# Moving the two layers' input tiles to the right end of SBUF, behind a 96-byte pad

## The chip, the cores and the metric

One core of a Trainium2 chip runs the kernel. The metric is device time in microseconds for one execution. The kernel before took 782.60, 784.05 and 780.63 us in three runs, so its median is 782.6 us. The profile is of one further execution.

## What is computed

Clustered attention, then two dense two-matrix layers. q, k and v have 2 batches, 8 heads, 768 positions and 64 values per head; 16 centroids per head decide which key a query may see.

```python
mask = q_assign[:, :, :, None] == k_assign[:, :, None, :]      # nearest centroid of q and of k
scores = np.where(mask, scale * np.matmul(q, k.transpose(0, 1, 3, 2)), -1e9)
attn = softmax(scores)
x = np.matmul(attn, v)            # laid out as [1536 tokens, 512]
h = x @ w_in                      # layer 0: 512 -> 2048
x = softplus(h) @ w_out           #          2048 -> 512
h = x @ w_in2                     # layer 1
out = (h * clip(h + 3, 0, 6) / 6) @ w_out2
```

The weights arrive as 64-bit floats and the kernel turns them into pairs of 32-bit numbers. Inputs of products are held as a high and a low part (`hi`, `lo`), and each product is the sum of three matmuls: hi by hi, lo by hi, hi by lo.

## The kernel before, in words

**Attention** (lines 173 to 846) goes over 8 pairs of heads, 12 tiles of 128 queries each. For each pair TensorE first makes the similarities to the centroids (`p_sims`, L308: 12 matmuls of 384 columns into `psm`; the stationary operand is a 128-column slice of `cwh` or `cwl`, the moving one half of `hiq`, `loq`, `hik` or `lok`). Then, tile by tile, come the scores (L408), the transposes (L438) and the product with v (L453). The order of everything is written out by hand (`at(step, place, function)`), inside `tc.manual_schedule()`. The result lands in the eight tiles `xhi0..3` and `xlo0..3` (L73, L74), each 128 partitions by 1536 floats: the layers' inputs.

**The layers** go over 2 layers x 3 blocks of 512 tokens (`tb`) x 16 slices of 128 hidden units (`f`). One step is an h group (`phase_a`, L169: 4 x 3 = 12 matmuls of 512 columns; stationary the weight slice `pi` of this f, moving `xhi` or `xlo`) and then the y group of two steps earlier (`phase_b`, 12 matmuls of 512 columns). In layer 0 (L898) the y group has the weight slice `po` as stationary operand and `ghi`, `glo` (the activations) as moving one; in layer 1 (L900) it is the other way round, with `po` moving. So TensorE's order is h(f), y(f-2), h(f+1), y(f-1) and so on. VectorE and ScalarE convert the weights of each f about two steps ahead in layer 0 (L109 to L144), and during the last block of layer 0 and the start of layer 1 for layer 1.

**Where tiles lie.** A tile pool takes its space as a stack, from the left (low addresses) or, with `side="right"`, from the right end. The offsets in each partition that the allocator gives are these; the last column is the offset modulo 64 bytes, called the phase below.

| tiles | opened at | side | bytes from .. to | phase |
|---|---|---|---|---|
| `ident` and small constants | L58 | left | 16,512 .. 17,408 | 0 for `ident` |
| `xhi0..3`, `xlo0..3`, 6,144 each | L59 | left | 17,408 .. 66,560 | 0 |
| weights f = 0..2 (`wpa`), 4,096 a tile | L61 | left | 66,560 .. 91,136 | 0 |
| `ghi`, `glo`, `g`, `u` | L852 | left, after attention | 91,136 .. 113,664 | 0 |
| weights f = 7..15 (`wpc`) | L854 | left, after attention | 121,856 .. 195,584 | 0 |
| Q, K, `pr`, `vs`, `pth`, `ptl` | L178 to L181 | left, attention | 91,136 .. 171,008 | 0 |
| `cwh`, `cwl` | L224, L225 | left, attention | 191,200 .. 192,992 | 32 |
| `hiq`, `loq` (two buffers each) | L177 | right, attention | 195,552 .. 207,840 | 32 |
| `hik`, `lok` (two buffers each) | L177 | right, attention | 207,840 .. 220,128 | 32 |
| q, k, v as loaded | L176 | right, attention | 220,128 .. 229,344 | 32 |
| weights f = 3..6 (`wpb`) | L626 | right, once q, k, v are done | 196,576 .. 229,344 | 32 |

The right end is at byte 229,344, whose remainder by 64 is 32. All sizes of the large tiles are multiples of 64, so everything that is stacked from the right has phase 32.

GpSimd (POOL) fills constants first: the identity (`make_identity`, L64), `tiew` (L71, 16 memsets), `cwh`, `cwl`; TensorE's first work, 15 warm-up transposes (L245), waits for the identity.

Of the kernel before, what the change touches and what calls it, by code (L numbers as in the profile page):

```python
# [8 lines left out]
F32 = mybir.dt.float32  # L9
# [13 lines left out]
def cluster_attention_then_two_mlps(  # L23
# [12 lines left out]
    nc = tc.nc  # L36
    P = 128
# [18 lines left out]

    nc.scalar.preload_act_table_set("natural_log_exp_and_others")
    const = ctx.enter_context(tc.tile_pool(name="const", bufs=1))  # L58
    xpool = ctx.enter_context(tc.tile_pool(name="x", bufs=1))  # L59
    NFA, NFB = 3, 7  # L60
    wpa = ctx.enter_context(tc.tile_pool(name="wpa", bufs=1))  # L61

# [968 lines left out]
```

## Time and profile before

| what | value |
|---|---|
| median of three runs | 782.6 us (780.63 to 784.05) |
| span of the profiled execution | 782.9 us |
| TensorE busy, of the span | 765.8 us, 98% |
| VectorE, ScalarE, GpSimd busy | 457.5, 410.0, 150.6 us |
| granted TensorE clock, mean | 0.998 |

The page has busy times of each engine, the busy share in 40 slices, the DMA queues, the chain of work that ended last, and the costliest groups of instructions. A matmul's recorded duration overlaps the next one, because matmuls are pipelined: what one of them costs in a stream is the distance from its start to the next start. In the chain of waits, which is cut into pieces that follow one another, the length of a piece "x12" is therefore the cost of 12 matmuls.

### The profile page before, as it was taken

To read this page: it belongs to the slowest core of one execution; us is meant where nothing else is said; L and a number is where in the kernel's file an instruction comes from. 1 tells how busy PE (TensorE), PEld (TensorE's weight loads), DVE (VectorE), ACT (ScalarE), POOL (GpSimd) and SP (SyncE) were. 2 spreads that over 40 slices of the span, in tenths; PEclk is the share of its full clock that TensorE was granted. 3 is DMA by queue.
4 is the path that set the end of the run, shared out by engine and by line. 5 is a ranking of instruction groups with operands and counts; after the bars stand their busy time and mean duration, and the time that the engine had idled before them with its cause. 6 is when DMAs were issued, how large, how long until landed. Compare 5 with 4: busy or idle time off the path is not lost.

```text
span 782.9 us, 10593 instructions
## 1 busy us (share of the span) xinstructions
PE 765.8 (98%) x3841; PEld 645.2 (82%) x3841; DVE 457.5 (58%) x788; ACT 410.0 (52%) x815; POOL 150.6 (19%) x222
## 2 busy tenths in 40 slices
PE   7979999999999999999999999999999999999998
PEld 6778898899888788888888888888888888888886
DVE  5969889889888999721111276779842322232221
ACT  6869889888998766532121344546532322222222
POOL 3467568667444000000000000000000000000000
PEclk9999999999999999999999999999999999999999
DMA  6645676676573670000000355640000100010001
GB/s 189 171 128 135 175 193 170 160 191 158 113 202 119 220 285 1 1 1 0 1 1 27 108 192 184 206 144 0 1 1 0 54 1 0 1 54 0 1 1 54
DMA packets 40548, 71.32 MB, mean 91 GB/s; under 512 B 4752, under 2 KB 25648, under 8 KB 40496
## 3 DMA queue, kind: packets, MB, share of 16 engines
q1 hardware_dynamic: 40352, 70.52, 31.2%
q8 instruction: 30, 0.49, 0.3%
q14 instruction: 22, 0.18, 0.1%
q10 hardware_dynamic: 144, 0.13, 0.0%
HBM read 46.30 MB, written 3.19 MB: 63 GB/s over the span
## 4 chain that ended last, share of the span: by engine, by line
PE 88%; DVE 3%; DMA 2%; ACT 2%; POOL 2%; issue 1%; SPq 1%; POOLq 0%; ACTq 0%
PE h L169 32%; PE y L900 17%; PE y L898 16%; PE t L438 7%; PE pv L453 7%; PE s L408 6%; PE psm L308 2%; DMA row<-rT 1%; DVE nm L416 1%; DVE ptl L443 1%; DMA rsb<-row 1%; ACT pth L442 0%; DMA K<-lok 0%; PE warm L245 0%; DMA K<-hik 0%
## 5 line engine op out<-in xcount | busy, mean ns | idle before, releaser
L169 PE MATMUL h<-xhi,pi 128*128 128x512 f32 x768 | 238.5, 392 | 0.7 <-DVE pi L144 0.6
L169 PEld LDWEIGHTS h<-xhi,pi 128*128 128x128 f32 x768 | 143.7, 188 | 32.4 <-DVE pi L144 1.0
L879 DVE TENSOR_TENSOR glo<-g,ghi 128x512 fp32r<-128x512 f32 x96 | 66.4, 692 | 146.2 <-ACT ghi L866 117.4
L169 PE MATMUL h<-xlo,pi 128*128 128x512 f32 x384 | 150.0, 391 | 0.0
L900 PE MATMUL y<-po,ghi 128*128 128x512 f32 x384 | 118.9, 391 | 0.0
L898 PE MATMUL y<-ghi,po 128*128 128x512 f32 x384 | 118.8, 391 | 0.0
L443 DVE TENSOR_TENSOR ptl<-t,pth 128x384 fp32r<-128x384 f32 x192 | 97.7, 550 | 24.1 <-ACT pth L442 23.1
L872 DVE SCALAR_TENSOR_TENSOR g<-u,h 128x512 f32<-128x512 f32 x48 | 33.0, 687 | 127.2 <-ACT u L868 127.1
L868 ACT ACTIVATE u<-h,half 128x512 f32<-128x512 f32 x48 | 33.0, 687 | 128.3 <-PE h L169 128.0
L408 PE MATMUL s<-K,Q 128*128 128x256 f32 (+1 forms) x384 | 90.3, 356 | 6.5 <-ACT pr L424 3.9
L442 ACT ACTIVATE pth<-t 128x384 fp32r<-128x384 f32 x192 | 85.8, 491 | 15.6 <-PE t L438 14.7
L416 DVE TENSOR_REDUCE nm<-s 128x1 f32<-128x768 f32 x96 | 90.7, 945 | 2.9 <-PE s L408 2.9
L424 ACT ACTIVATE pr<-s,nm 128x768 f32<-128x768 f32 x96 | 86.9, 905 | 3.2 <-DVE nm L416 2.9
L438 PE MATMUL t<-ident,pr 128*128 128x128 f32 x576 | 85.9, 279 | 2.2 <-DVE ptl L443 1.8
L865 ACT ACTIVATE g<-h 128x512 f32<-128x512 f32 x48 | 28.5, 595 | 111.1 <-PE h L169 111.1
L169 PEld LDWEIGHTS h<-xlo,pi 128*128 128x128 f32 x384 | 72.0, 188 | 15.7
L900 PEld LDWEIGHTS y<-po,ghi 128*128 128x128 f32 x384 | 72.1, 188 | 15.6
L898 PEld LDWEIGHTS y<-ghi,po 128*128 128x128 f32 x384 | 72.0, 188 | 15.7
L408 PEld LDWEIGHTS s<-K,Q 128*128 128x128 f32 x384 | 65.8, 189 | 16.7 <-ACT pr L424 5.2
L438 PEld LDWEIGHTS t<-ident,pr 128*128 128x128 f32 x576 | 66.4, 141 | 15.7 <-DVE ptl L443 11.8
L900 PE MATMUL y<-po,glo 128*128 128x512 f32 x192 | 75.1, 391 | 0.0
L898 PE MATMUL y<-glo,po 128*128 128x512 f32 x192 | 75.0, 391 | 0.0
(126 smaller groups left out, 933.6 us busy)
## 6 DMA issues: line engine op xcount, KB each, us to landing
ri<-in_moe_w_in SPq DMA_DIRECT2D x29, 512.0 KB, 4.6
ro<-in_moe_w_out SPq DMA_DIRECT2D x29, 512.0 KB, 8.0
K<-hik SPq DMA_DIRECT2D x31, 192.0 KB, 5.1
Q<-hiq SPq DMA_DIRECT2D x15, 384.0 KB, 4.0
Q<-loq SPq DMA_DIRECT2D x16, 192.0 KB, 5.5
v<-in_v SPq DMA_DIRECT2D x8, 384.0 KB
rsb<-row SPq DMA_DIRECT2D x16, 192.0 KB, 3.9
K<-lok SPq DMA_DIRECT2D x15, 192.0 KB, 4.3
```

Of the source, the lines that this page charges most:

```text
L169: nc.tensor.matmul(hs[n][:, :TB], w[:, c, :], x[c][:, cols], start=(c == 0 and i == 0), stop=(c == NC - 1 and i == 2))
L408: nc.tensor.matmul(ps[:, n0:n1], Q[i][:, u, j * P:(j + 1) * P], K[i][:, u, n0:n1], start=(u == 0), stop=(u == 1),)
L416: nc.vector.tensor_reduce(nm, st_s[t][:, :S], AX.X, ALU.max, negate=True)
L424: nc.scalar.activation(pr, st_s.pop(t)[:, :S], AF.Exp, bias=st_p[t], accum_out=sums_of[n][:, i, j:j + 1])
L438: nc.tensor.transpose(pt[:, c * P:(c + 1) * P], pr[:, kt * P:(kt + 1) * P], ident)
L442: last_flip[:] = [nc.scalar.activation(dh, src, AF.Copy)]
L443: nc.vector.tensor_tensor(dl, src, f32(dh), ALU.subtract)
L453: nc.tensor.matmul(st_v[h][:, :HALF], vs[:, kt, i, :], st_t[h][u][:, kt, :], start=(kt == 0 and u == 0), stop=(kt == NJ - 1 and u == 1),)
L868: nc.scalar.activation(t["u"], t["h"], AF.Relu, bias=half, scale=1.0 / 6.0)
L879: nc.vector.tensor_tensor(t["glo"], t["g"], f32(t["ghi"]), ALU.subtract)
L898: nc.tensor.matmul(y[:, :TB], w[:, e, :], x, **fl)
L900: nc.tensor.matmul(y, x[:, e * P:(e + 1) * P], w.rearrange("p c e -> p (c e)"), **fl)
```

## The change

Two pools are opened on the right side at the start: `edge`, with one tile of 128 x 24 floats (96 bytes a partition) that only one memset of a single column touches, and then the layers' inputs, which lay on the left before. No other line changes.

```diff
     const = ctx.enter_context(tc.tile_pool(name="const", bufs=1))
-    xpool = ctx.enter_context(tc.tile_pool(name="x", bufs=1))
+    edge = ctx.enter_context(tc.tile_pool(name="edge", bufs=1, side="right"))
+    pad = edge.tile([P, 24], F32, name="pad")
+    nc.gpsimd.memset(pad[:, :1], 0.0)
+    xpool = ctx.enter_context(tc.tile_pool(name="x", bufs=1, side="right"))
     NFA, NFB = 3, 7
```

By the stack rule the tiles then lie so (each offset is one of the table above, less 49,152 on the left, and less 49,152 + 96 for what was on the right):

| tiles | bytes from | phase |
|---|---|---|
| pad | 229,248 | 0 |
| `xhi0..3`, `xlo0..3` | 180,096 (to 229,248) | 0 |
| weights f = 0..2, 7..15 | 17,408 and 72,704 | 0 |
| weights f = 3..6 | 147,328 | 0 |
| `hiq`, `loq`, `hik`, `lok` | 146,304 | 0 |
| `cwh`, `cwl` | 142,048 | 32 |

## Rows read from the trace of the kernel before

**Rows 1.** The page: its first line.

```profile
span 782.9 us, 10593 instructions
```

**Rows 2.** The page, part 4: the chain that ended last, by engine and by line.

```profile
PE 88%; DVE 3%; DMA 2%; ACT 2%; POOL 2%; issue 1%; SPq 1%; POOLq 0%; ACTq 0%
PE h L169 32%; PE y L900 17%; PE y L898 16%; PE t L438 7%; PE pv L453 7%; PE s L408 6%; PE psm L308 2%; DMA row<-rT 1%; DVE nm L416 1%; DVE ptl L443 1%; DMA rsb<-row 1%; ACT pth L442 0%; DMA K<-lok 0%; PE warm L245 0%; DMA K<-hik 0%
```

**Rows 3.** The chain in order of time: start us, us, what.

```profile
32.73 3.57 DMA K<-lok
...
269.22 2.82 PE h L169 x11
...
274.77 2.80 PE h L169 x12
...
521.33 2.72 PE h L169 x12
524.05 2.73 PE y L900 x12
526.77 2.79 PE h L169 x12
...
540.61 2.80 PE y L900 x12
...
549.01 2.75 PE h L169 x12
...
732.82 2.80 PE y L900 x12
...
771.01 8.17 PE y L900 x36
```

**Rows 4.** Timeline of PE, 136 to 141 us: start us, us, what.

```profile
137.04 0.33 PE L308 MATMUL psm<-hiq,cwl 128*128 128x384 f32 x1
137.21 0.33 PE L308 MATMUL psm<-hik,cwh 128*128 128x384 f32 x1
137.38 0.34 PE L308 MATMUL psm<-lok,cwh 128*128 128x384 f32 x1
137.56 0.34 PE L308 MATMUL psm<-hik,cwl 128*128 128x384 f32 x1
137.73 0.85 PE L408 MATMUL s<-K,Q 128*128 128x512 f32 x4
...
138.77 0.34 PE L453 MATMUL pv<-pth,vs 128*128 128x384 f32 x1
138.94 0.34 PE L453 MATMUL pv<-ptl,vs 128*128 128x384 f32 x1
139.12 0.34 PE L308 MATMUL psm<-hiq,cwh 128*128 128x384 f32 x1
139.29 0.34 PE L308 MATMUL psm<-loq,cwh 128*128 128x384 f32 x1
139.47 0.34 PE L308 MATMUL psm<-hiq,cwl 128*128 128x384 f32 x1
```

**Rows 5.** Line 123, VectorE, by operand: count, then ns min/median/max.

```profile
L123 DVE SCALAR_TENSOR_TENSOR val<-ri,val x32: 677/685/693, 36.1 to 572.2; 128x512 uint32<-128x512 uint32 x32
```

**Rows 6.** Timeline of all engines, 273.5 to 279 us.

```profile
273.62 0.69 DVE L144 TENSOR_TENSOR pi<-val,pi 128x512 fp32r<-128x512 f32 x1
...
274.61 0.63 PE L169 MATMUL h<-xhi,pi 128*128 128x512 f32 x2
...
278.76 0.68 DVE L144 TENSOR_TENSOR pi<-val,pi 128x512 fp32r<-128x512 f32 x1
```

**Rows 7.** Windows: us, then busy us of each engine, clock, DMA share, GB/s.

```profile
136.60:164.80 28.20, 28.19 (x191) 25.61 (x189) 24.38 (x43) 25.01 (x58) 20.19 (x27) 1.00 0.69 169
```

**Rows 8.** Timeline of all engines, 0 to 2.3 us.

```profile
0.87 0.59 POOL L71 MEMSET tiew<- 128x1 f32 x16
...
2.06 0.47 PE L245 MATMUL warm<-ident 128*128 128x128 f32 x1 [2.06 <-POOL ident masks.py:199]
```

## The prediction

> **What bounds the kernel now.** I read the page first: the profiled execution spans 782.9 us [rows 1], and TensorE holds 88% of the chain that ended last, 65% of it in the layers' h and y groups [rows 2]. The sum below is made against this execution; the median of the runs is 0.3 us under it, so I take the sum off 782.6. Next I read the chain in order of time. From 269 us to the end it is nothing but groups of 12 matmuls, h and y in turn, with no other engine between them, up to the last 36 [rows 3]. The reader is to see there that equal groups do not cost the same. The h group at 521.33 takes 2.72 us, the one at 526.77 takes 2.79, the y group at 540.61 takes 2.80. Counting steps of two groups from the start of the block, 526.77 is f = 3 and 540.61 is the y group of f = 3, two steps later. All slow groups are of f = 3 to 6, in both layers and all blocks: 46 pieces of 2.79 or 2.80 us between those at 274.77 and 732.82 [rows 3] (48 would be all; the h groups of f = 3 and 4 in the first block lie where weights are still awaited). They are the slices whose weights lie in the right-hand pool, at phase 32, while everything that meets them lies at phase 0. It makes no difference whether the weights are the stationary operand (h, and y of layer 0) or the moving one (y of layer 1): 0.08 us over 12 matmuls, 6.7 ns each.
>
> Is it the phase or the place? The trace has a pair that separates the two. In attention, `cwh` and `cwl` lie at phase 32 and so do the tiles that move past them. Three successive `psm` matmuls start 0.17 us apart, as do the `pv` matmuls of the same 384 columns whose operands are all at phase 0 [rows 4]. So two operands that are both at phase 32 cost nothing extra, although `hik` lies over 207,000 bytes. What the slow groups have alone is two operands of different phase. This is my reading: **unequal phases cost some 6.7 ns a matmul**.
>
> **The change part by part.**
>
> *Weights f = 3 to 6 go from phase 32 to 0.* Every operand of the layers is then at phase 0. On the chain from 271.9 us on, 22 groups of 2.79 lose 0.07, 24 of 2.80 lose 0.08, nine h groups of f = 7 to 9 in layer 1, which follow a slow y group and take 2.75 (the one at 549.01), lose 0.03, and 22 of 2.73 lose 0.01 against 2.72 [rows 3]: 1.54 + 1.92 + 0.27 + 0.22 = 3.95 us. The 11 matmuls at 269.22, f = 4, add 0.07: **-4.0 us**. Before 269 us these savings don't count, since TensorE awaits weights there. Does a faster TensorE run into the conversion of weights again? For f = 5 VectorE ends at 274.31 and TensorE begins at 274.61; its next slice comes 5.14 us later [rows 6], while two groups at 2.72 take 5.44, so VectorE draws ahead by 0.3 us a step. At f = 5 the slack of 0.30 us loses the 0.07 gained on f = 4, and afterwards it grows. If VectorE did catch it, the loss would be within the 0.5 us gained up to f = 7.
>
> *`hiq`, `loq`, `hik`, `lok` go from phase 32 to 0, but `cwh` and `cwl` stay at 32*, for 49,152 is a multiple of 64. The 96 `psm` matmuls then have what the slow groups have now. The trace does not show this pairing; the nearest rows are the h groups of f = 3 to 6 (stationary at 32, moving at 0), 6.7 ns each, and that I take. The lower end is nothing, which the change of phase from `psm` to `s` at 137.56, still 0.17 us, would speak for [rows 4]. TensorE is busy for 28.19 of 28.20 us in a steady pair [rows 7], so nothing covers it there: 6 pairs x 12 x 6.7 ns = **+0.5 us**. In the first two pairs other engines hold much of the chain; I count those 24 as hidden, and 0.2 us if not. The range is 0 to +0.7.
>
> *One memset more on GpSimd*, ahead of the identity for which TensorE's first transpose waits [rows 8]. Sixteen of the same width take 0.59 us, 0.04 each; the bounds are 0 and 0.1. All of GpSimd's queue comes later by this, the `cwh` fill too, and TensorE with it: **+0.04**.
>
> *Everything else that moves.* VectorE's conversions read and write slices of both phases, and 32 of them lie between 677 and 693 ns [rows 5], so I cost other engines' operands at 0. Transfers out of `lok` and the like start from another offset; the one that stands on the chain takes 3.57 us [rows 3], and nothing here shows it from phase 0. I take 0 and allow 0.3 us either way for such transfers. The order of instructions and which tile takes over whose space stay as they are, since the left stack and the right stack each move as a whole.
>
> Sum: -4.0 + 0.5 + 0.04 = -3.5 us; 782.6 becomes **779.1 us**, 0.45% less.
>
> A rule of the Trainium skill would have it otherwise. SBUF — State Buffer (Specifications) gives SBUF lines of 16 bytes, and every tile here starts on a multiple of 32, so by that page the move would shift nothing: the sum would be the memset alone, 782.6. The trace disagrees, with 2.80 against 2.72 us for like groups [rows 3].
>
> **The rivals.**
>
> *A: place, not phase.* Reads beyond some address near 196,000 are slow: f = 15 ends at 195,584 and is fast, f = 3 starts at 196,576 and is slow. Then the weights are cured (-4.0), but the new x reaches beyond it: `xhi3` and all of `xlo` and, in the last block, `xhi2`, that is 6 of 12 matmuls of an h group in two blocks and 8 in the third. 96 h groups x 6.7 matmuls x 6.7 ns = +4.3. With the memset the time is 782.9. For it: nothing slow in the layers lies lower. Against it: `hik` lies there and is not slow [rows 4]. The same time comes out if operands' addresses don't matter at all and f = 3 to 6 are slow for another reason, such as what was converted when. Against that: in both layers the same four are slow, though their weights are other ones.
>
> *B: a wider period, the slower side.* If the two operands must agree modulo 256 bytes and not 64, the change makes new mismatches: x and the weights f = 3 to 6 come to 128 modulo 256, while the weights of the other 12 slices and the activations stay at 0. The place is the h groups of 12 slices in 6 blocks, 72 groups, which are fast now: 72 x 0.08 = +5.8. The y groups of f = 3 to 6 stay slow, so of the 4.0 only some 2.0 comes back; with +0.5 it is +4.3, **786.9 us**. It decides as soon as a difference of 128 bytes counts as one of 32 does. Against it: `hiq` and its slice of `cwh` stand 128 apart modulo 256 and `hik` and its slice 0, and both are 0.17 to 0.18 us apart [rows 4]. For it: no stream of the layers has such a pair.
>
> **How the numbers follow.** 0.5%, 3.9 us, is about what a measurement of this kernel can tell from no change. Phase as forecast: 0.70, with 778.4 to 779.8 for the unknown costs (`psm` free, or all of it on the path and the transfers worse) and about 1 us of spread between runs. Rival A and its like: 0.17. Rival B: 0.13. The forecast lies 0.4 us short of 778.7, where "faster" begins, so I give 0.30 of its 0.70 to faster and 0.40 to same; A adds 0.14 to same and 0.02 to faster on its edges, and 0.01 to slower. Faster 0.32, same 0.54, slower 0.14. The range leaves out B and the outermost runs: 777.5 to 783.5. The likeliest case's own range is 778 to 780.5.
>
> **What the profile would show.** Right: all pieces of 12 from 275 us on at 2.72 or 2.73, f = 3 to 6 too; the last 36 still 8.17; `psm` starts some 0.18 us apart in place of 0.17. Rival A: h groups of all f near 2.76, y groups all at 2.72. Rival B: h groups of 2.80 for f = 0 to 2 and 7 to 15, and 2.72 for f = 3 to 6. The prediction is wrong if slow groups appear in the steady stretch elsewhere than in `psm`, or if attention ends at another time than some 0.5 us later.

## The result, and the profile after

The kernel after takes 783.65 us (median of 14 runs, 782.76 to 788.84), the kernel before, on the same chip and beside it, 779.53 us (14 runs). The ratio is 1.006, with a 95% interval of 1.0043 to 1.0077: the change costs 4.1 us. (The ratios in this document are estimates over the runs, not the quotient of the two medians, which is 1.0053 here.) The prediction said 3.5 us less, from a median of 782.6 in the first three runs, with a range of 777.5 to 783.5, so sign and range are both wrong; as that median lay 3.1 us higher, it is compared by differences below. What happened is its rival B, a period of 256 bytes, which it had priced at +4.3 us and given a chance of 0.13.

The profiled execution of before, whose rows stand above, was a long one: its third pair of heads reaches its `psm` matmuls at 51.34 us, that of after at 45.64. Its span is thus the longer of the two although the kernel is the faster, and only stages are compared here. The page of after, its first line, its line of busy times and the two rows of the chain by engine and by line [rows 1, 2]:

```profile
span 781.3 us, 10594 instructions
PE 767.5 (98%) x3841; PEld 642.3 (82%) x3841; DVE 458.5 (59%) x788; ACT 410.1 (52%) x815; POOL 150.9 (19%) x223
PE 87%; DVE 4%; ACT 3%; DMA 3%; issue 1%; POOL 1%; SPq 0%; POOLq 0%; ACTq 0%; DVEq 0%
PE h L172 33%; PE y L903 17%; PE y L901 16%; PE t L441 7%; PE s L411 6%; PE pv L456 6%; PE psm L311 2%; DMA rsb<-row 1%; DVE nm L419 1%; DVE ptl L446 1%; DMA row<-rT 1%; ACT pth L445 1%; ACT pr L427 1%; DMA q<-in_q 0%; PE pbk L324 0%
```

Nothing new bounds the kernel: TensorE does the same 3841 matmuls and is busy 1.7 us longer with them (765.8 before). Lines stand three further down (h is L172, y L901 and L903). The chain of after in order of time, from the change of layers on (506.78 is h of f = 0 in layer 1, 523.37 is f = 3, 537.02 the y group of f = 3, 567.58 h of f = 11), beside [rows 3]:

```profile
263.46 2.82 PE h L172 x11
...
329.93 2.79 PE h L172 x12
...
506.78 2.79 PE h L172 x12
509.57 2.73 PE y L901 x12
...
523.37 2.73 PE h L172 x12
...
537.02 2.80 PE y L903 x12
...
567.58 2.79 PE h L172 x12
570.37 2.73 PE y L903 x12
...
769.35 8.19 PE y L903 x36
```

In before, h of f = 0 in block 1 of layer 0 is

```profile
335.09 2.72 PE h L169 x12
```

The pattern of the h groups has turned over. Before, h groups were fast at f = 0 to 2 and 7 to 15 and slow at 3 to 6; now the twelve are slow (some 2.79) and the four are fast (2.73), as rival B had said of the profile. The y groups of f = 3 to 6 are as slow as they were. Read to the nanosecond from the starts of the matmuls, from h of f = 5 in the first block on, where TensorE no longer waits for weights: 69 h groups of the twelve slices cost 4.69 us more in sum, 22 h groups of the four 1.34 less, 24 y groups of the four 0.12 less, and 68 y groups of the twelve, most of them beside slow h groups now, 0.89 more, 13 ns each: +4.12 us.

That accounts for the whole difference, as far as one profiled execution of each can. In the chain, the row at 329.93 is h of f = 0 in block 1 of layer 0; from there to the end are 781.26 - 329.93 = 451.33 us, in before 782.89 - 335.09 = 447.80: +3.53. In the first block, from the 11 matmuls of f = 4 (263.46; 269.22 in [rows 3]) to that point, it is 66.47 against 65.87: +0.60. Together it is +4.13, and the medians differ by 4.12.

### The profile page after: what moved, and what is told of

Same layout as the page of the kernel before. It is cut to its first block, busy times and chain, and to the rows that moved or that the text cites. A ratio compares the mean times of both kernels' runs of the same rounds, so it can differ in the third digit from the quotient of the medians.

```text
span 781.3 us, 10594 instructions
## 1 busy us (share of the span) xinstructions
PE 767.5 (98%) x3841; PEld 642.3 (82%) x3841; DVE 458.5 (59%) x788; ACT 410.1 (52%) x815; POOL 150.9 (19%) x223
## 4 chain that ended last, share of the span: by engine, by line
PE 87%; DVE 4%; ACT 3%; DMA 3%; issue 1%; POOL 1%; SPq 0%; POOLq 0%; ACTq 0%; DVEq 0%
PE h L172 33%; PE y L903 17%; PE y L901 16%; PE t L441 7%; PE s L411 6%; PE pv L456 6%; PE psm L311 2%; DMA rsb<-row 1%; DVE nm L419 1%; DVE ptl L446 1%; DMA row<-rT 1%; ACT pth L445 1%; ACT pr L427 1%; DMA q<-in_q 0%; PE pbk L324 0%
## 5 line engine op out<-in xcount | busy, mean ns | idle before, releaser
L172 PE MATMUL h<-xhi,pi 128*128 128x512 f32 x768 | 240.4, 394 | 0.8 <-DVE pi L147 0.8
L172 PEld LDWEIGHTS h<-xhi,pi 128*128 128x128 f32 x768 | 143.9, 188 | 33.9 <-DVE pi L147 1.2
L172 PE MATMUL h<-xlo,pi 128*128 128x512 f32 x384 | 151.3, 394 | 0.0
L903 PE MATMUL y<-po,ghi 128*128 128x512 f32 x384 | 119.2, 391 | 0.0
L901 PE MATMUL y<-ghi,po 128*128 128x512 f32 x384 | 119.1, 391 | 0.0
L172 PEld LDWEIGHTS h<-xlo,pi 128*128 128x128 f32 x384 | 72.1, 188 | 16.8
L901 PEld LDWEIGHTS y<-ghi,po 128*128 128x128 f32 x384 | 72.1, 188 | 16.3
L903 PEld LDWEIGHTS y<-po,ghi 128*128 128x128 f32 x384 | 72.2, 188 | 16.1
L901 PE MATMUL y<-glo,po 128*128 128x512 f32 x192 | 75.1, 391 | 0.0
L903 PE MATMUL y<-po,glo 128*128 128x512 f32 x192 | 75.1, 391 | 0.0
```

The costliest lines, as they stand in the source:

```text
L172: nc.tensor.matmul(hs[n][:, :TB], w[:, c, :], x[c][:, cols], start=(c == 0 and i == 0), stop=(c == NC - 1 and i == 2))
L901: nc.tensor.matmul(y[:, :TB], w[:, e, :], x, **fl)
L903: nc.tensor.matmul(y, x[:, e * P:(e + 1) * P], w.rearrange("p c e -> p (c e)"), **fl)
```

## The experiments

**What was to be told apart.** Which quantity of the two operands makes a group slow: the place in SBUF (rival A), a difference modulo 64 bytes (the prediction), modulo 256 (rival B), modulo 512, or that an operand is not aligned? The first four runs move x, and what is stacked from the right, one at a time. Their offsets modulo 256 (weights of the other slices, `ghi` and `glo` stay at 0):

| kernel | x | weights f = 3 to 6 |
|---|---|---|
| before | 0 | 224 |
| after | 128 | 128 |
| e1: x right, pad 224 | 0 | 0 |
| e2: x left, pad 224 on the right | 0 | 0 (256 modulo 512) |
| e3: x left, pad 96 on the right | 0 | 128 (0 modulo 64) |
| e4: x right, no pad | 224 | 224 |

e3 to e8 have one run each, the profiled one. In e1 and e2 the profiled run was the longest of six (778.94 and 778.75), so a single time says little, and these kernels are read by stretches of their chains.

**e1**, the change with another pad:

```diff
-    pad = edge.tile([P, 24], F32, name="pad")
+    pad = edge.tile([P, 56], F32, name="pad")
```

> The changed kernel with a pad of 224 bytes in place of 96: x and the weights f = 3 to 6 come to 0 modulo 256, like all the rest. Theory M (the two operands of a 512-column matmul must agree modulo 256 bytes, else it costs some 6 ns): every group of 12 takes 2.72 us, the layers lose the 4.0 us that the kernel before has over that, ratio to before 0.995. Theory P (x is slow because of where it lies, above byte 180,000): the h groups of f = 0 to 2 and 7 to 15 stay at 2.79, ratio 1.001 to 1.006. Theory M512 (they must agree modulo 512; x lies at 256 modulo 512): as the changed kernel, ratio 1.006.

Measured: 776.59 us (6 runs, 774.05 to 778.94) against 779.56 (11 runs), ratio 0.9939, 0.9916 to 0.9962. Its chain, at the same groups as above:

```profile
267.40 2.83 PE h L172 x11
...
332.79 2.72 PE h L172 x12
...
523.19 2.72 PE h L172 x12
...
536.79 2.72 PE y L903 x12
...
765.26 8.17 PE y L903 x36
```

No group of the steady stretch is slow any more. From 332.79 to the end (777.16) it is 444.37 us, 3.43 less than before, and 65.39 from the f = 4 row to there, 0.48 less: -3.9 in the layers. Since x and the weights f = 3 to 6 lie at the right end as in after, the place makes nothing slow.

**e2**, before with the pad alone:

```diff
+    edge = ctx.enter_context(tc.tile_pool(name="edge", bufs=1, side="right"))
+    pad = edge.tile([P, 56], F32, name="pad")
+    nc.gpsimd.memset(pad[:, :1], 0.0)
     xpool = ctx.enter_context(tc.tile_pool(name="x", bufs=1))
```

> x stays on the left as in the kernel before; only a pad of 224 bytes stands at the right end, which brings the weights f = 3 to 6 to 0 modulo 256 (256 modulo 512). Theory M: groups of f = 3 to 6 at 2.72, ratio to before 0.995. Theory M512: these groups stay at 2.79 to 2.80, ratio 1.000. Theory P says here that the weights above byte 196,000 stay slow, ratio 1.000.

Measured: 774.97 us (6 runs, 774.26 to 778.75), ratio 0.9936, 0.9914 to 0.9959. Every steady group takes 2.72, h and y of f = 3 in layer 1 among them:

```profile
522.96 2.72 PE h L172 x12
...
536.56 2.72 PE y L903 x12
```

Weights at 256 and x at 0 modulo 512 are as fast as equal ones, so a difference of 256 counts for nothing. Moving x is not needed: this kernel and e1 beat both before and after, and their intervals do not tell them apart.

**e3**, as e2 with 24 floats in place of 56.

> x stays on the left; only the pad of 96 bytes stands at the right end, so the weights f = 3 to 6 lie at 0 modulo 64 and 128 modulo 256. The step of the prediction (64 bytes decide): f = 3 to 6 at 2.72 us, 4.0 us less than before. Theory M: f = 3 to 6 stay at 2.79 to 2.80 in h and y, time as before.

Measured: one run, 782.25 us. This is the run that decides against the prediction's own reading, for every operand of the layers is at 0 modulo 64 here. Its chain at h of f = 0 in block 1 of layer 0, then h of f = 3 and the y groups of f = 3 to 5 in layer 1:

```profile
332.49 2.72 PE h L172 x12
...
524.38 2.80 PE h L172 x12
...
538.28 2.77 PE y L903 x12
...
543.85 2.80 PE y L903 x12
...
549.38 2.79 PE y L903 x12
```

f = 3 to 6 are as slow as in before; from h of f = 0 in block 1 to the end it is 780.45 - 332.49 = 447.96 us, in before 447.80. Phase 0 modulo 64 cures nothing here.

**e4**, the change without pad and memset, x on the right:

```diff
-    xpool = ctx.enter_context(tc.tile_pool(name="x", bufs=1))
+    xpool = ctx.enter_context(tc.tile_pool(name="x", bufs=1, side="right"))
```

> x on the right with no pad: x and the weights f = 3 to 6 at 224 modulo 256, the rest at 0. Theory M: the h groups of the 12 other slices at 2.79 to 2.80, the h groups of f = 3 to 6 near 2.72, the y groups of f = 3 to 6 at 2.79: 4 us more than before, as with the 96 bytes. The step of the prediction says the same here (32 modulo 64), so this run shows only what the pad is worth: under M nothing, under the step of the prediction 4 us and more.

Measured: one run, 790.84 us. x and the four slices now agree at 224, all else is at 0:

```profile
336.10 2.80 PE h L169 x12
338.90 2.75 PE y L898 x12
...
513.67 2.80 PE h L169 x12
...
530.32 2.75 PE h L169 x12
...
544.09 2.79 PE y L900 x12
```

The same pattern as after, a little dearer: 2.80 for the twelve h groups, and 2.75 for the groups after them, where after has 2.73. From the h group of block 1 (336.10) to the end, 789.07, it is 452.97 us, 1.64 more than after and 5.17 more than before. The whole is 11.3 us over the median of before, where 4 were expected; what goes beyond the 5.17 lies ahead of these groups, in one execution, and is not explained. So the 96 bytes of the change alter the price of a mismatch, not its place.

**e5 and e6, a staircase of offsets.** 32 bytes more behind each of the eight tiles of f = 3 to 6 set every slice at another offset, in before's layout; e6 has besides a pad of 8 floats at the right, which shifts all by 32.

```diff
+    def slot(f, pool, dt, tag, name):
+        more = 8 if NFA <= f < NFB else 0
+        return pool.tile([P, 8 * P + more], dt, tag=tag, name=name)[:, :8 * P]
...
-        w = pool.tile([P, 2, NC, P], F32R, tag=f"w{nm}{f}", name=f"p{nm}{f}")
+        w = slot(f, pool, F32R, f"w{nm}{f}", f"p{nm}{f}").rearrange("p (h c e) -> p h c e", h=2, c=NC)
```

> The kernel before, with 32 bytes more behind each weight tile of f = 3 to 6, so that its eight tiles stand at eight offsets modulo 256: pi of f = 3, 4, 5, 6 at 224, 32, 96, 160 and po at 0, 64, 128, 192; all else at 0. Theory M: only the y groups of f = 3 are cured (2.72 to 2.73 us), all other groups of f = 3 to 6 take 2.77 to 2.80 whatever the offset. If the cost grows with the distance modulo 256, the groups at 128, 96 and 160 cost more than those at 224 and 32. Step of the prediction (64 bytes decide): y groups of f = 3 to 6 all at 2.72, h groups all slow.

> The same staircase 32 bytes lower: pi of f = 3 to 6 at 192, 0, 64, 128 and po at 224, 32, 96, 160. Theory M: only the h groups of f = 4 are cured, all others of f = 3 to 6 take 2.77 to 2.80. Step of the prediction: all h groups of f = 3 to 6 at 2.72, all their y groups slow.

Measured: one run each, 781.11 and 781.28 us. In e5 the slices `pi` of f = 3 to 6 are at 224, 32, 96, 160 and `po` at 0, 64, 128, 192; in e6 `pi` at 192, 0, 64, 128 and `po` at 224, 32, 96, 160. The chain of e5 in block 1 of layer 0, first the h groups of f = 3, 4, 5, then the y group of f = 3, h of f = 6 and the y groups of f = 4, 5, 6:

```profile
348.21 2.79 PE h L173 x12
...
353.74 2.79 PE h L173 x12
...
359.26 2.81 PE h L173 x12
362.06 2.74 PE y L902 x12
364.80 2.80 PE h L173 x12
367.60 2.80 PE y L902 x12
...
373.14 2.80 PE y L902 x12
...
378.69 2.75 PE y L902 x12
```

The same groups in e6, h of f = 3, 4, 5, then y of f = 3, h of f = 6 and y of f = 4:

```profile
348.60 2.75 PE h L176 x12
...
354.07 2.72 PE h L176 x12
...
359.51 2.80 PE h L176 x12
362.31 2.79 PE y L905 x12
365.10 2.79 PE h L176 x12
367.89 2.80 PE y L905 x12
```

In e6 the h group of f = 4, the one at 0, takes 2.72 between h groups of f = 3 and 5 at 2.75 and 2.80; in e5 the y group of f = 3 at 0 takes 2.74 between two slow ones. Read to the nanosecond from the starts of the matmuls, over both layers and over e3 to e6 and after, the excess of a group over 2,720 ns by its difference (offset of the stationary operand less that of the moving one, modulo 256) is:

| difference | excess of a group, ns |
|---|---|
| 0 | 0, up to 50 beside slow groups |
| 32 | 70 to 83 |
| 64 | 78 to 80 |
| 96 | 85 to 89 |
| 128 | 55 to 77 |
| 160 | 78 to 95 |
| 192 | 27 to 35 |
| 224 | 70 to 83 |

So all but 0 cost, some 5 to 8 ns a matmul, with one exception that none of the readings had: a stationary operand 64 bytes below the moving one costs only 27 to 35 ns a group. It is the difference with its sign, for +64 has the full price. Which operand the weights are changes less: at 160 the excess is 78 to 80 with the weights stationary and 95 with them moving.

**e7, does attention pay it too?** A tile of 128 bytes between Q and K, and one between `vs` and `pth`, `ptl`, so that K and Q, and `vs` and `pth` or `ptl`, stand 128 apart where they agreed:

```diff
+            gap_p = pool("gap", 1)
...
+            nc.gpsimd.memset(gap_p.tile([P, 32], F32, name="gap_v")[:, :1], 0.0)
...
+            gap_k = qk.tile([P, 32], F32, name="gap_k")
+            nc.gpsimd.memset(gap_k[:, :1], 0.0)
```

> The kernel before with two gaps of 128 bytes in attention: K stands at 128 and Q at 0 modulo 256 (scores, L408: two matmuls of 512 and two of 256 columns a tile), vs at 128 and pth, ptl at 0 (product with v, L453: 384 columns). If theory M holds for any number of columns, pv starts 180 ns apart in place of 173 and the four scores of a tile take 0.71 us in place of 0.69. If matmuls of 384 columns are spared, as the psm rows would then have been, pv stays at 173 ns and only the two of 512 columns pay.

Measured: one run, 784.45 us. A part of the timeline of PE:

```profile
131.56 0.34 PE L457 MATMUL pv<-pth,vs 128*128 128x384 f32 x1
131.74 0.34 PE L457 MATMUL pv<-ptl,vs 128*128 128x384 f32 x1
131.92 0.34 PE L457 MATMUL pv<-pth,vs 128*128 128x384 f32 x1
132.09 0.34 PE L457 MATMUL pv<-ptl,vs 128*128 128x384 f32 x1
```

The starts are still 0.17 to 0.18 us apart, and in rows of two decimals no cost is to be seen. Over the 264 `pv` matmuls from 60 to 215 us the mean distance rises from 176.6 ns in before to 178.1 (from 174.4 to 176.6 where the next one is a `pv` too), 1.5 to 2.2 ns each, and a steady pair of heads takes 28.27 us or a little more where it took 28.20. In e1, whose `pv` operands agree, that mean is 177.2, so a part of the 1.5 is scatter. In the short runs of attention a difference of 128 costs a third of what it costs in the layers or less. The distances of the scores, of 512 and 256 columns, hardly changed (193.5 to 193.3 ns). The first tile moves `pr` as well; the mean distance of the transposes that read it stays at 119.8 ns.

**e8, fewer columns in the same long stream.** Before with blocks of 384 tokens in place of 512; offsets as in before. It computes in four blocks instead of three, with more matmuls (4417), so its time of 805.5 us is no verdict on anything but the size of a group.

```diff
-    TB = 512
+    TB = 384
...
-        for e, y in enumerate(ys):
+        for e, y in enumerate(ys if layer == 0 else ys[:TB // P]):
```

> The kernel before with 4 blocks of 384 tokens in place of 3 of 512; offsets modulo 256 are those of the kernel before. The h groups and the y groups of layer 0 then have 384 columns, the y groups of layer 1 (9 matmuls) still 512. If 384 columns are spared: groups of 12 at 2.08 us for all f, f = 3 to 6 too, and the y groups of layer 1 at 2.04 us but 2.10 for f = 3 to 6. If 384 columns pay as well: f = 3 to 6 at 2.15 to 2.16 in h, in layer 0 and 1. The time of the whole is longer, since there are more matmuls.

Its chain, second block of layer 0, h of f = 3 and 4 and the y group of f = 3 (416.15), with neighbours:

```profile
405.63 2.12 PE h L169 x12
407.75 2.08 PE y L898 x12
409.83 2.12 PE h L169 x12
...
416.15 2.12 PE y L898 x12
...
430.91 2.08 PE h L169 x12
```

2.12 against 2.08 us: 3.3 ns a matmul at 384 columns, half of what 512 columns pay. Layer 1 of this kernel gave no clear picture: there the h groups of f = 10 to 15 take 2.11 us too, though their operands agree by these offsets, and that stays open.

**e9, agreement or alignment?** All that lies on the left is shifted by 224 bytes, so x, all weights and the activations stand at 224, where f = 3 to 6 are in before:

```diff
+    shift = ctx.enter_context(tc.tile_pool(name="shift", bufs=1))
+    gap = shift.tile([P, 56], F32, name="gap")
+    nc.gpsimd.memset(gap[:, :1], 0.0)
     xpool = ctx.enter_context(tc.tile_pool(name="x", bufs=1))
```

> A pad of 224 bytes on the left, ahead of x, nothing on the right: x, all weights, the activations and attention's large tiles stand at 224 modulo 256, so every pair of operands in the layers agrees, and none is a multiple of 64. Theory M (only the difference modulo 256 counts): all groups at 2.72 to 2.73 us, ratio 0.994 to 0.995, as with the pad of 224 on the right. Theory A (each operand must itself start on a multiple of 256): all groups at 2.79 or more, ratio 1.012 or more.

Measured: 778.45 us (median of 12 runs, of which one is a stray of 1,962.57) against 779.72 (17 runs), ratio 0.9970, 0.9954 to 0.9986. Its chain:

```profile
332.59 2.72 PE h L172 x12
...
522.99 2.72 PE h L172 x12
...
536.59 2.72 PE y L903 x12
```

Every steady group takes 2.72, f = 3 to 6 among them (522.99 and 536.59 are h and y of f = 3 in layer 1), and from 332.59 to the end (777.40) it is 444.81 us, 2.99 less than before. The 0.44 us by which e1 is shorter lie almost wholly behind the start of the last matmul. No operand of the layers stands on a multiple of 256, or of 64: what counts is that the two agree. Why the whole gains less, 1.3 us by the medians and 2.3 by the ratio, is not settled. Attention shows 28.24 us a pair against 28.20, which over six pairs is 0.2 us of it.

## Why the prediction was wrong

**The step that failed** is the one that turned the `psm` rows [rows 4] into a rule. From starts 0.17 to 0.18 us apart it read that `hiq` and its slice of `cwh`, which stand 128 apart modulo 256, cost nothing, and set the period of the pattern at 64 bytes. e3 shows otherwise: 0 modulo 64 with 128 modulo 256 takes 2.80 (its h group at 524.38). The rows could not bear the conclusion. They are of 384 columns in runs of a few matmuls, and the cost there is 3.3 ns in a long stream (e8) and some 2 in short runs (e7), where the layers have 6 to 7; rows with steps of 10 ns show neither. Read to the nanosecond, from 60 to 215 us of the same trace, `hiq` with its slice of `cwh` is followed after 172 or 173 ns, `loq` with the same slice after 175 to 180, and the agreeing `hik` and `lok` after 173 or 174 (a first one behind a transpose, after 259 or 260 in both cases): a few nanoseconds at one place and nothing at the other. So a finer view of these rows would not have settled it either. A near zero in short runs was taken for a rule of the long stream, and the only evidence against rival B was that.

- *Place or phase:* right against place. e1 has the right end in use and every group at 2.72. That the two operands' offsets must agree, and not be aligned, was right as well (e9).
- *"Every operand of the layers is then at phase 0", -4.0 us:* the size was right for a true cure: e1's layers are 3.9 us shorter. But the change does not cure. It puts x and the four slices at 128 modulo 256 and leaves the rest at 0, so the cure reaches only the 24 h groups in which those two meet.
- *What the sum left out:* the h groups of the other slices, +4.7 us for the 69 that the chain has, and +0.9 for their neighbours. Rival B had the first at +5.8, the cure of the h groups of f = 3 to 6 at -2.0 (measured -1.3) and `psm` at +0.5 (about 0), and did not have the second. Its mechanism was right; that its +4.3 lies so near the measured +4.1 is in part luck.
- *`psm`, +0.5 us:* mis-sized. Between 60 and 215 us the mean distance between successive `psm` matmuls is 174.1 ns in after and 174.3 in before, and a pair takes 28.19 us against 28.20 [rows 7]; the term measured about 0, its lower end. The rate of 6.7 ns was carried from 512 columns in a long stream to short runs of 384.
- *The memset, +0.04:* right. TensorE's first transpose starts at 2.09 us in after, e1 and e2 and at 2.06 in before [rows 8], 0.03 later. *The transfers, 0 +- 0.3,* were not measured by themselves.
- *VectorE's conversions at 0:* the first block of e1 is 0.48 us shorter and its chain has no VectorE piece there; TensorE did not run into them.
- *16-byte lines:* the prediction weighed a statement of the Trainium skill, SBUF — State Buffer (Specifications), that SBUF has lines of 16 bytes, and drew from it that this move would shift nothing. The traces disagree with what it drew: every difference tried but 0 costs a group 27 to 95 ns.

**What the mechanism may be** is in part argued. The starts do show which two reads meet: that of the moving operand of the running matmul and that of the next one's weights, which are loaded while it runs. In before, the load for h of f = 3 in block 1 starts with the last matmul of the y group ahead of it:

```profile
351.02 0.40 PE L898 MATMUL y<-glo,po 128*128 128x512 f32 x1
351.02 0.42 PEld L169 LDWEIGHTS h<-xhi,pi 128*128 128x128 f32 x2
```

That y group agrees in itself and takes 226 or 227 ns a matmul, but 235 for this last one; the last matmul of the slow h group, under which agreeing weights are loaded, takes 227. In after, from block 1 of layer 0 on, at the 25 places where two groups that agree in themselves follow each other, but the moving operand of the first and the weights of the second stand 128 apart, the last distance of the first is 232 or 233 ns. At the 46 places where the first group agrees in itself and the next one does not, but its weights agree with the operand still running, it is 226 or 227.

The Trainium skill, TensorE: Matmul & The Clock Gate (Part 2: What happens when you issue a matmul), gives TensorE two independent read ports and says that loading the next weights doesn't steal read bandwidth from the running matmul. Groups that differ in the offsets alone take 2.79 and 2.72 us here, so in this kernel the two reads are not independent of their addresses. Why they meet at a period of 256, why -64 is cheap, why short runs pay less, and why a mismatch is dearer in e4 than in after stays open.

## What to carry to other kernels

List the offsets of every stationary and moving tile modulo 256, not only modulo 64, before moving a pool: in long streams of wide 32-bit matmuls like these the two should agree, and here a pad of 224 bytes ahead of the first right-hand tile made them (0.994 of the time) while one of 96 did not. Look for such a cost in the length of whole groups of equal matmuls, since a row of two decimals hides a few nanoseconds, and don't let a rival fall on rows of another stage, with other widths and shorter runs, that might not have shown it.

## What the runs showed of the hardware that was not expected

- The price of two operands depends on the difference of their offsets modulo 256, in steps of 32 at the finest tried: 55 to 95 ns in 2,720 for most, 27 to 35 at 192, none at 0 or 256.
- What meets is the running matmul's moving operand and the next one's weights, so a mismatch costs the group ahead of it as well (235 ns for its last matmul in before). Behind a slow group, too, a group that agrees can lose time in its first matmuls (some 232 ns in place of 227 for the first three of y groups in after). Together it is up to 50 ns a group.
- The cost falls faster than the width: some 6 ns at 512 columns, 3.3 at 384.
